# A chunked state-space scan that feeds a two-layer product: chunks of 64 tokens instead of 128, weight conversion on three engines, second product two groups behind

## The chip, the core and the metric

One core of a Trainium2 chip runs the whole program. TensorE (PE in the profile; PEld is its weight load) multiplies, VectorE (DVE), ScalarE (ACT) and GpSimd (POOL) work elementwise, and SyncE (SP) issues most of the DMA transfers. The metric is the device time of one execution in microseconds, lower is better.

## The reference

The first half is a scan with a decaying state (batch 4, 8 heads, 768 tokens, 32 channels per head, 16 states), here for one head:

```python
cum = np.cumsum(np.log(a))                       # within a chunk
M = (C @ B.T) * exp(cum[i] - cum[j]) * (i >= j)
y = M @ x + (C @ state) * exp(cum)
state = exp(cum[-1]) * state + (B * exp(cum[-1] - cum)).T @ x
```

The heads of a token are put side by side, which gives 3072 tokens of 256 channels, and the second half is a product with SiLU between its two layers:

```python
h = y @ w_in                   # 256 -> 2048
out = (h / (1 + exp(-h))) @ w_out   # 2048 -> 256
```

The result does not depend on the length of the chunks. All inputs are fp32 except the two weight matrices, which reach the chip as float64 and are rounded to fp32 on it. All products are fp32; the profile has two matmul records for each matmul instruction (one for each transpose).

## The kernel before, in words

Everything stays on the chip between the two halves. Tokens are worked on in groups of 256, twelve in all, three to a batch. The line numbers are those of the kernel before.

**The scan.** A group is two chunks of 128 tokens. Once per batch, `prep_decay` and `prep_T` bring B and C of 768 tokens into layouts with states on the partitions (`bh`, `ce`, `cw`), and `prep_N` brings B back to tokens on partitions (`bn`). B and C are loaded with six consecutive tokens on a partition, so GpSimd first sorts them (L224), PE transposes twelve blocks (L232), the copies put tokens in order, and six more transposes follow (L261). Per chunk there are four pieces. `f_E` (DVE, L268 and L271) makes the decays E between all pairs of tokens by one scan over 8 heads x 128 tokens on 128 partitions. `f_G` multiplies C and B for four pairs of heads on four row tiles of the PE array (L283), and DVE multiplies the result with E (M, L287). `f_D` forms the chunk's part of the state (L306, four column tiles), and DVE adds it to the decayed state and spreads it by a mask (L313, L317). `f_Y` multiplies the state (L326) and M (L334) into y, which ACT copies to XM (L339).

**The two layers.** `f_s1(g, j)` makes two of sixteen blocks of h (four matmuls, L352) in one of the two PSUM slots named `hp` and ACT applies SiLU (L354). `f_s2(g, j)` adds four of the sixteen blocks to an output tile (four matmuls, L361), and after each fourth call ACT copies the tile out (L365).

**The weights.** Sixteen pieces (eight of w_in, then eight of w_out) come in by DMA as pairs of 32-bit words. For each, `w_size` runs six instructions on DVE (L137 to L146) and one addition on GpSimd (L147), and `w_sign` one more on DVE (L153). Four pieces can be in flight; the load of piece n + 4 is issued after the last step of piece n.

**Order.** The order is written out by hand; no scheduler changes it, and each engine takes its instructions in program order. The loop at the end of the kernel runs over g = -1 to 12 and j = 0 to 7 and issues in each step: layer one of group g, preparation of a later batch, layer two of group g - 1, a piece of the scan of group g + 1, a piece of `f_E` or `f_B` of group g + 2, and, while g is below 1, the next weight piece. So all sixteen pieces are converted during g = -1 and g = 0, and layer one of group 0 shares DVE's queue with half of them.

Of the kernel before, what the change touches and what calls it, by code (L numbers as in the profile page):

```python
# [13 lines left out]
# as fp32, the bits of float64's high word for 2^-127 and for 2^128 * (1 - 2^-20)  # L14
# [5 lines left out]
def kernel(  # L20
# [22 lines left out]
    Q = 128  # L43
    CPB = S // Q
    NCH = batch * CPB
    R = S // 128
# [3 lines left out]
    GC = 2  # L50
    GT = GC * Q
    NG = NCH // GC
    GPB = CPB // GC
    assert (H * N, H * D, D, N) == (128, 256, 32, 16) and CPB % GC == 0 and d_model == H * D

    const = ctx.enter_context(tc.tile_pool(name="const", bufs=1))
    bcp = ctx.enter_context(tc.tile_pool(name="bcp", bufs=2))
    bcr = ctx.enter_context(tc.tile_pool(name="bcr", bufs=1))
    xp = ctx.enter_context(tc.tile_pool(name="xp", bufs=8))
    abp = ctx.enter_context(tc.tile_pool(name="abp", bufs=3))  # L60
    rawp = ctx.enter_context(tc.tile_pool(name="rawp", bufs=4))
    wtp = ctx.enter_context(tc.tile_pool(name="wtp", bufs=2))
    bat = ctx.enter_context(tc.tile_pool(name="bat", bufs=2))
    epool = ctx.enter_context(tc.tile_pool(name="epool", bufs=3))
    mpool = ctx.enter_context(tc.tile_pool(name="mpool", bufs=2))
    st = ctx.enter_context(tc.tile_pool(name="st", bufs=2))
    xmp = ctx.enter_context(tc.tile_pool(name="xmp", bufs=2))
    gpool = ctx.enter_context(tc.tile_pool(name="gpool", bufs=2))
    opool = ctx.enter_context(tc.tile_pool(name="opool", bufs=3))
    ps_g = ctx.enter_context(tc.tile_pool(name="ps_g", bufs=1, space=bass.MemoryType.PSUM))  # L70
    ps_y = ctx.enter_context(tc.tile_pool(name="ps_y", bufs=1, space=bass.MemoryType.PSUM))
    ps_h = ctx.enter_context(tc.tile_pool(name="ps_h", bufs=2, space=bass.MemoryType.PSUM))
    ps_o = ctx.enter_context(tc.tile_pool(name="ps_o", bufs=1, space=bass.MemoryType.PSUM))
# [4 lines left out]
    pa, bc, xt, ab = {}, {}, {}, {}  # L78
    RAW = 4

    def load_batch(b, q0, q1):
        # a of a batch, each head on the N partitions of its states
        pa[b] = bat.tile([128, S], FP32, name="pa")
        q0.dma_start(out=pa[b], in_=bass.AP(tensor=a.tensor, offset=a.offset + b * H * S,
                                            ap=[[S, H], [0, N], [1, S]]))
        # token p * R + r of a batch on partition p: runs of R * N elements
        bc[b] = bcp.tile([128, 2, H, R * N], FP32, name="bc")
        for i, q in ((0, q0), (1, q1)):
            q.dma_start(out=bc[b][:, i], in_=(B, C)[i][b].rearrange("h (p r) n -> p h (r n)", r=R))

    def load_a(gc):
        # a of a chunk on all partitions
        b, c = divmod(gc, CPB)
        ab[gc] = abp.tile([128, H, Q], FP32, name="ab")
        nc.sync.dma_start(out=ab[gc], in_=bass.AP(tensor=a.tensor, offset=a.offset + b * H * S + c * Q,
                                                  ap=[[0, 128], [S, H], [1, Q]]))

    def load_x(gc):
        b, c = divmod(gc, CPB)
        xt[gc] = xp.tile([128, H, D], FP32, name="xt")  # L100
        nc.sync.dma_start(out=xt[gc], in_=x[b, :, c * Q:(c + 1) * Q, :].rearrange("h p d -> p h d"))
# [6 lines left out]
    raw = {}  # L108

    def w_piece(which, j):  # L110
# [4 lines left out]
    def load_w(which, j, q):  # L115
        src, dst = w_piece(which, j)
        if src.dtype == FP32:
            q.dma_start(out=dst, in_=src)
            return
        t = raw[which, j] = rawp.tile([128, 2, 2 * WF], U32, name="raw")  # L120
        q.dma_start(out=t, in_=src.bitcast(U32))

    # float64 as (low, high) words to fp32
    def w_parts(n):
        w = raw[W[n]].rearrange("p k (f two) -> p k f two", two=2)
        return w[:, :, :, 0], w[:, :, :, 1]

    def w_size(n):
        if W[n] not in raw:
            return  # L130
        lo, hi = w_parts(n)
        t = wt[n] = wtp.tile([128, 2, WF], U32, name="wt")
        r = wtp.tile([128, 2, WF], U32, name="wr")
        tf, rf = t.bitcast(FP32), r.bitcast(FP32)
        # the high word's magnitude orders as an fp32 number of its bits, so comparing it as one holds
        # it in fp32's range of exponents: below comes zero, above the largest numbers
        nc.vector.tensor_scalar(out=t, in0=hi, scalar1=0x7FFFFFFF, scalar2=None, op0=ALU.bitwise_and)  # L137
# [3 lines left out]
        nc.vector.tensor_scalar(out=t, in0=t, scalar1=4, scalar2=1,  # L141
                                op0=ALU.logical_shift_left, op1=ALU.logical_shift_right)
        nc.vector.tensor_scalar(out=t, in0=t, scalar1=0x40000000, scalar2=None, op0=ALU.bitwise_xor)  # L143
        # the low word's part: low * 2^-52 of the power of two
        nc.vector.tensor_scalar(out=r, in0=t, scalar1=0x7F800000, scalar2=None, op0=ALU.bitwise_and)  # L145
        nc.vector.scalar_tensor_tensor(out=rf, in0=lo, scalar=2.0 ** -52, in1=rf, op0=ALU.mult, op1=ALU.mult)  # L146
        nc.gpsimd.tensor_tensor(out=tf, in0=tf, in1=rf, op=ALU.add)  # L147

    def w_sign(n):
        if W[n] in raw:  # L150
            lo, hi = w_parts(n)
            dst = w_piece(*W[n])[1]
            nc.vector.scalar_tensor_tensor(out=dst.bitcast(U32), in0=hi, scalar=0x80000000, in1=wt.pop(n),  # L153
                                           op0=ALU.bitwise_and, op1=ALU.bitwise_or)
        if n + RAW < len(W):
            load_w(*W[n + RAW], nc.sync)
# [288 lines left out]
```

## Time and profile before

| | us |
|---|---|
| median of three runs | 487.18 (486.95 to 487.48) |
| span of the profiled execution, first to last instruction | 484.2 |
| median of the runs above that span | 3.0 |
| PE busy | 410.2 (85% of the span) |
| DVE busy | 207.2 (43%) |
| ACT busy | 87.7 (18%) |
| POOL busy | 60.6 (13%) |

The profile is of one execution, whose own time is known as its span; what lies around the span (3.0 us, if this execution was a median one) is carried unchanged through the prediction. Busy shares are averages over the span: what an engine is worth is read from the stage in which it is the last to finish. Times are in microseconds unless marked ns. In a row of the timeline the first number is the start from the span's start, the second how long the group of instructions lasted, and `xN` the number of records in it.

### The profile page before, as it was taken

The numbers are of one execution on the slowest core, as the hardware profiler recorded it, in microseconds if no ns is written. First come the engines' busy times: TensorE is split into PE (matmuls) and PEld (weight loads), VectorE is DVE, ScalarE is ACT, GpSimd is POOL, SyncE is SP. The second block draws the span as 40 slices with busy tenths as digits, with TensorE's granted clock in tenths as the row PEclk, the third lists the DMA queues.
The fourth block names the chain that finished last, engine by engine and source line by source line (L and its number), as shares of the span: only waits on it lengthen the run. The fifth ranks groups of instructions, "written<-read, shape, count | busy, mean of one in ns | idle before, by whom it ended". The sixth has DMA issues, their size and how long they took to land.

```text
span 484.2 us, 5726 instructions
## 1 busy us (share of the span) xinstructions
PE 410.2 (85%) x2424; PEld 333.0 (69%) x2424; DVE 207.2 (43%) x258; ACT 87.7 (18%) x162; POOL 60.6 (13%) x89
## 2 busy tenths in 40 slices
PE   0421816456999999999999999999999999999996
PEld 0210514345887787888878888888878778788885
DVE  2999999997703414528034036172250341100000
ACT  1200201011221121122212212222112121212110
POOL 6022342234200000300100003002000000000000
PEclk9999969597999999999999999999999999999999
DMA  9994434310271302202704022022010000000000
GB/s 195 272 242 136 131 111 126 125 51 1 70 159 35 88 11 67 54 12 65 153 12 110 21 54 66 12 65 56 11 56 11 1 12 11 11 2 12 11 12 22
DMA packets 66617, 32.35 MB, mean 67 GB/s; under 512 B 34336, under 2 KB 61984, under 8 KB 66592
## 3 DMA queue, kind: packets, MB, share of 16 engines
q1 hardware_dynamic: 65552, 31.59, 25.3%
q10 hardware_dynamic: 1040, 0.39, 0.3%
q8 instruction: 19, 0.31, 0.3%
q14 instruction: 6, 0.05, 0.0%
HBM read 28.84 MB, written 3.15 MB: 66 GB/s over the span
## 4 chain that ended last, share of the span: by engine, by line
PE 76%; DVE 18%; issue 2%; DMA 2%; POOL 1%; ACT 0%; SPq 0%; ACTq 0%; POOLq 0%
PE o_ps L361 34%; PE hp L352 33%; DVE E L271 3%; DVE wt L137 3%; PE gram L283 3%; PE yb L334 2%; PE yb L326 2%; DMA bc<-in_B_dram 2%; DVE wt L138 2%; DVE wr L145 1%; DVE wt L141 1%; DVE wt L143 1%; DVE w_in_sb L153 1%; DVE SP L317 1%; DVE w_out_sb L153 1%
## 5 line engine op out<-in xcount | busy, mean ns | idle before, releaser
L352 PE MATMUL hp<-XM,w_in_sb 128*128 128x256 f32 x768 | 191.8, 394 | 0.5 <-ACT XM L339 0.5
L361 PE MATMUL o_ps<-w_out_sb,gT 128*128 128x256 f32 x768 | 181.7, 381 | 1.0 <-ACT o_sb L365 1.0
L352 PEld LDWEIGHTS hp<-XM,w_in_sb 128*128 128x128 f32 x768 | 143.5, 193 | 32.5 <-issue 9.0
L361 PEld LDWEIGHTS o_ps<-w_out_sb,gT 128*128 128x128 f32 x768 | 145.4, 191 | 21.1 <-ACT o_sb L365 1.8
L354 ACT ACTIVATE gT<-hp 128x512 f32<-128x512 f32 x96 | 57.3, 597 | 231.3 <-PE hp L352 231.3
L287 DVE TENSOR_TENSOR M<-gram,E 128x1024 f32<-128x1024 f32 x24 | 29.3, 1219 | 162.8 <-PE gram L283 162.8
L271 DVE TENSOR_TENSOR_SCAN E<-ab,ident 128x1024 f32<-128x1024 f32 x24 | 56.6, 2358 | 5.8 <-POOL ab L269 5.8
L326 PE MATMUL yb<-cw,SP 128*128 128x128 f32 x80 | 14.0, 302 | 38.5 <-DVE SN L313 38.5
L326 PEld LDWEIGHTS yb<-cw,SP 128*128 128x128 f32 x80 | 13.0, 211 | 40.4 <-DVE SN L313 39.5
L269 POOL MEMSET ab<- 128x8 f32 x24 | 2.7, 112 | 252.9 <-DVE ab L268 252.9
L147 POOL TENSOR_TENSOR wt<-wt,wr 128x512 f32<-128x512 f32 x16 | 25.1, 1566 | 57.3 <-DVE wr L146 57.3
L232 PE MATMUL hp<-ident,br 128*128 128x128 f32 x48 | 9.0, 325 | 20.7 <-POOL br L224 20.4
L339 ACT ACTIVATE XM<-yb 128x256 f32<-128x256 f32 x24 | 9.2, 383 | 95.4 <-PE yb L334 95.4
L232 PEld LDWEIGHTS hp<-ident,br 128*128 128x128 f32 x48 | 6.9, 166 | 22.4 <-POOL br L224 20.8
L334 PE MATMUL yb<-M,xt 128*32 128x128 f32 x384 | 17.2, 302 | 5.9 <-DVE SN L311 5.9
L283 PE MATMUL gram<-ce,bh 32*128 32x256 f32 x192 | 18.7, 460 | 0.0
L365 ACT ACTIVATE o_sb<-o_ps 128x256 f32<-128x256 f32 x24 | 9.2, 383 | 41.7 <-PE o_ps L361 39.4
L334 PEld LDWEIGHTS yb<-M,xt 128*32 128x32 f32 x384 | 9.9, 117 | 9.9 <-DVE SN L311 6.1
L268 DVE TENSOR_SCALAR ab<-ab 128x1024 f32<-128x1024 f32 x24 | 16.4, 684 | 0.4 <-DMA ab<-in_a_dram 0.4
L248 DVE TENSOR_SCALAR ce<-hp,par 128x256 f32<-128x256 f32 (+1 forms) x16 | 12.7, 875 | 6.1 <-PE hp L232 6.1
L296 POOL TENSOR_TENSOR BT<-bn,E 128x128 f32<-128x128 f32 x20 | 13.4, 678 | 10.7 <-DVE SN L313 6.9
L137 DVE TENSOR_SCALAR wt<-raw 128x512 uint32<-128x512 uint32 x16 | 14.2, 890 | 0.3
(36 smaller groups left out, 144.8 us busy)
## 6 DMA issues: line engine op xcount, KB each, us to landing
ab<-in_a_dram SPq DMA_DIRECT2D x24, 512.0 KB, 4.1
raw<-in_moe_w_in_dram SPq DMA_DIRECT2D x8, 512.0 KB, 5.1
raw<-in_moe_w_out_dram SPq DMA_DIRECT2D x8, 512.0 KB, 3.6
xt<-in_x_dram SPq DMA_DIRECT2D x24, 128.0 KB, 4.1
out_dram<-o_sb SPq DMA_DIRECT2D x24, 128.0 KB, 1.7
pa<-in_a_dram SPq DMA_DIRECT2D x4, 384.0 KB
bc<-in_B_dram SPq DMA_DIRECT2D x4, 384.0 KB, 8.3
bc<-in_C_dram SPq DMA_DIRECT2D x3, 384.0 KB, 8.5
```

Of the source, the lines that this page charges most:

```text
L137: nc.vector.tensor_scalar(out=t, in0=hi, scalar1=0x7FFFFFFF, scalar2=None, op0=ALU.bitwise_and)
L147: nc.gpsimd.tensor_tensor(out=tf, in0=tf, in1=rf, op=ALU.add)
L232: nc.tensor.transpose(out=tp[:, s * 128:(s + 1) * 128], in_=d["br"][:, i, r].rearrange("p h n -> p (h n)"), identity=ident)
L268: nc.vector.tensor_scalar(out=t, in0=t, scalar1=1.0, scalar2=1e-6, op0=ALU.min, op1=ALU.max)
L271: nc.vector.tensor_tensor_scan(out=E[gc].rearrange("p h t -> p (h t)"), data0=t.rearrange("p h t -> p (h t)"), data1=ident8.rearrange("p h ...
L283: nc.tensor.matmul(out=gram[:, g, 0:256], lhsT=d["bh"][32 * g:32 * g + 32, cs], rhs=d["ce"][32 * g:32 * g + 32, :, cs], start=True, stop=True,
L287: nc.vector.tensor_tensor(out=M[gc], in0=gram[:, :, 0:256], in1=E[gc].rearrange("p (g e) t -> p g (e t)", e=2), op=ALU.mult)
L326: nc.tensor.matmul(out=y_ps[:, w], lhsT=sp[:, w * 128:(w + 1) * 128], rhs=U[b]["cw"][:, c * Q:(c + 1) * Q], start=(w == 0), stop=False, sk ...
L334: nc.tensor.matmul(out=y_ps[32 * k:32 * k + 32, w], lhsT=xc[:, h], rhs=m[:, h], start=(c == 0 and w == 0), stop=True, tile_position=(0, 32 ...
L352: nc.tensor.matmul(out=hp[:, i * GT:(i + 1) * GT], lhsT=w_in_sb[:, kc, f * 128:(f + 1) * 128], rhs=XM[g][:, kc, :], start=(kc == 0), stop= ...
L354: nc.scalar.activation(GTS[g][:, 2 * j:2 * j + 2].rearrange("p f t -> p (f t)"), hp, AF.Silu)
L361: nc.tensor.matmul(out=OPS[g], lhsT=GTS[g][:, f, tt * Q:(tt + 1) * Q], rhs=w_out_sb[:, f, :], start=(f == 0), stop=(f == NF - 1))
```

## The change

The whole scan and the weight conversion are rewritten; the two layers keep their matmuls.

- **Chunks of 64 tokens.** A unit of 256 tokens is four chunks; two chunks lie one above the other on the partitions (64 c, c = 0 or 1), two beside each other (k). `f_E` makes E for a unit with one scan over 2 x 8 x 64 elements, where the kernel before had two scans over 8 x 128. Each matmul of `f_G`, `f_D` and `f_Y` is cut in smaller ones: 16, 16 and 16 + 32 for a unit, with 64 or 128 columns, on tiles of 32 x 64 or 64 x 32 of the PE array.
- **Natural order.** B and C are loaded per unit with one token on a partition (runs of 64 bytes), so that four transposes per unit suffice (`f_T`); the sorting on GpSimd, the six transposes back and the per-batch preparation are gone. The copies behind the transposes move from DVE to ACT, but for `cw`.
- **Loads.** One unit is eleven DMAs, issued as a block by `load_unit` two units ahead. Of unit 0, B, C and x come through ACT's queue.
- **Weights.** Per piece two instructions on ACT, two on GpSimd and two on DVE, spread over three successive steps (`w_size`, `w_bits`, `w_sign`); five pieces can be in flight.
- **Order.** Layer two runs two groups behind layer one (LAG = 2). Unit 0 is scanned before the loop with pieces 0 to 3; the other pieces follow, one per step, until j = 5 of g = 1.
- **PSUM.** `gram` and `y` share four banks under one name (`gy`), `f_D` takes both `hp` slots, and the output tile has two slots instead of one.

```diff
-    Q = 128
+    Q = 64
+    UT = 256
...
+    LAG = 2
...
+    gpool = ctx.enter_context(tc.tile_pool(name="gpool", bufs=LAG + 1))
...
+        for t in range(4):
+            k, c = divmod(t, 2)
+            q.dma_start(out=ab[u][64 * c:64 * c + 64, k],
+                        in_=bass.AP(tensor=a.tensor, offset=a.offset + b * H * S + t0 + t * Q,
+                                    ap=[[0, 64], [S, H], [1, Q]]))
...
+            for k in range(2):
+                q.dma_start(out=bct[u][:, i, k],
+                            in_=(B, C)[i][b, :, t0 + 128 * k:t0 + 128 * k + 128].rearrange("h p n -> p h n"))
...
+            nc.scalar.activation(u, raw[n][:, :, :, 1].bitcast(FP32), AF.Abs)
...
+            nc.scalar.activation(v, raw[n][:, :, :, 0], AF.Copy, scale=2.0 ** -51, bias=2.0)
...
+            nc.gpsimd.tensor_scalar(out=u, in0=u, scalar1=LEAST, scalar2=MOST, op0=ALU.max, op1=ALU.min)
...
+    def w_bits(n):
...
+            nc.vector.tensor_scalar(out=u, in0=u, scalar1=3, scalar2=None, op0=ALU.logical_shift_left)
+            nc.gpsimd.tensor_tensor(out=v, in0=u, in1=v, op=ALU.add)
...
+            nc.vector.scalar_tensor_tensor(out=dst.bitcast(U32), in0=raw[n][:, :, :, 1], scalar=0x80000000,
+                                           in1=wv.pop(n).bitcast(U32), op0=ALU.bitwise_and, op1=ALU.bitwise_or)
...
+        if n < len(W):
+            w_size(n)
+        if 0 <= n - 1 < len(W):
+            w_bits(n - 1)
+        if 0 <= n - 2 < len(W):
+            w_sign(n - 2)
...
+        nc.scalar.activation(BH[u], tb, AF.Copy)
+        for e in range(2):
+            nc.scalar.activation(CE[u][:, e], tcc, AF.Copy, scale=par[:, e:e + 1])
+        nc.vector.tensor_tensor(out=CW[u], in0=tcc, in1=PFX[u], op=ALU.mult)
...
+                for g in range(4):
+                    nc.tensor.matmul(out=gram[64 * c:64 * c + 64, g, 128 * k:128 * k + 128],
+                                     lhsT=bh[32 * g:32 * g + 32, ts], rhs=ce[32 * g:32 * g + 32, :, ts],
+                                     start=True, stop=True, tile_position=(32 * g, 64 * c), skip_group_check=True)
...
+        dp = [ps_h.tile([128, 512], FP32, name="hp") for c in range(2)]
...
+                nc.tensor.matmul(out=dp[c][32 * g:32 * g + 32, 64 * k:64 * k + 64],
+                                 lhsT=bt[64 * c:64 * c + 64, k, 32 * g:32 * g + 32],
+                                 rhs=xc[64 * c:64 * c + 64, k, 64 * g:64 * g + 64], start=True, stop=True,
+                                 tile_position=(64 * c, 32 * g), skip_group_check=True)
...
+                nc.tensor.matmul(out=y[64 * q:64 * q + 64, 2 * w + c, 64 * k:64 * k + 64],
+                                 lhsT=sp[32 * g:32 * g + 32, t], rhs=cw[32 * g:32 * g + 32, Q * t:Q * t + Q],
...
+                        nc.tensor.matmul(out=y[32 * q:32 * q + 32, 2 * w + c, 64 * k:64 * k + 64],
+                                         lhsT=xc[64 * c:64 * c + 64, k, h], rhs=m[64 * c:64 * c + 64, k, h],
...
+    def scan_piece(u, j):
+        if j == 0:
+            f_P(u)
+            f_E(u)
+        elif j == 1:
+            f_T(u)
+            f_B(u)
+        elif j == 2:
+            f_G(u)
+        elif j == 4:
+            f_D(u)
         elif j == 6:
...
+            f_Y(u)
+        elif j == 7 and u + 2 < NU:
+            load_unit(u + 2)
...
+    for g in range(NU + LAG):
         for j in range(8):
...
+            if g < NU:
                 f_s1(g, j)
...
+                scan_piece(g + 1, j)
+            if 8 * g + j + 4 < len(W) + 2:
+                next_w(8 * g + j + 4)
+            if g >= LAG:
+                f_s2(g - LAG, j)
```

On PE, one group in the loop's steady part stood like this before (a row is the line, the tile written and the tiles read with their buffer numbers, the size of one, and the count of instructions; L352 is layer one, L361 layer two, the rest is the scan):

```order
L352 MATMUL hp_960<-XM_861,w_in_sb_111 128x256 x4
L361 MATMUL o_ps_966<-w_out_sb_112,gT_801 128x256 x4
L283 MATMUL gram_161<-ce_632,bh_631 128x256 x4
L352 MATMUL hp_977<-XM_861,w_in_sb_111 128x256 x4
L361 MATMUL o_ps_966<-w_out_sb_112,gT_801 128x256 x4
L306 MATMUL yb_162<-xt_463,BT_942 32x64 x4
L352 MATMUL hp_1001<-XM_861,w_in_sb_111 128x256 x4
L361 MATMUL o_ps_966<-w_out_sb_112,gT_801 128x256 x4
L326 MATMUL yb_162<-cw_633,SP_907 128x128 x2
L334 MATMUL yb_162<-M_975,xt_463 32x128 x8
```

The same place now, from j = 3 to j = 6 of a group (L339 is layer one, L350 layer two; `hp_887` and `hp_888` are the two slots of `f_D`):

```order
L339 MATMUL hp_867<-XM_770,w_in_sb_87 128x256 x4
L350 MATMUL o_ps_809<-w_out_sb_88,gT_317 128x256 x4
L339 MATMUL hp_881<-XM_770,w_in_sb_87 128x256 x4
L278 MATMUL hp_887<-xt_566,BT_832 32x64 x4
L278 MATMUL hp_888<-xt_566,BT_832 32x64 x4
L278 MATMUL hp_887<-xt_566,BT_832 32x64 x4
L278 MATMUL hp_888<-xt_566,BT_832 32x64 x4
L350 MATMUL o_ps_913<-w_out_sb_88,gT_317 128x256 x4
L339 MATMUL hp_918<-XM_770,w_in_sb_87 128x256 x4
L350 MATMUL o_ps_913<-w_out_sb_88,gT_317 128x256 x4
L339 MATMUL hp_928<-XM_770,w_in_sb_87 128x256 x4
L313 MATMUL gy_934<-cw_827,sp_911 64x64 x12
```

What a group ran as two rounds of three pieces is now one round of larger pieces with many more, smaller matmuls, and the state's piece stands directly behind a layer-one block and takes the `hp` slot that this block has just filled.

On DVE, one weight piece stood like this before, between the pieces ahead of and behind it (`wt` and `wr` are its work tiles, `raw` what came by DMA):

```order
L137 TENSOR_SCALAR wt_348<-raw_289 128x512
L138 TENSOR_SCALAR wt_348<-wt_348 128x512
L141 TENSOR_SCALAR wt_348<-wt_348 128x512
L143 TENSOR_SCALAR wt_348<-wt_348 128x512
L145 TENSOR_SCALAR wr_349<-wt_348 128x512
L146 SCALAR_TENSOR_TENSOR wr_349<-raw_289,wr_349 128x512
L153 SCALAR_TENSOR_TENSOR w_in_sb_111<-raw_265,wt_323 128x2x256
```

DVE's rows around the same pieces now (`wu` and `wv` are the work tiles; L249 is `cw`, L262 is M):

```order
L146 TENSOR_SCALAR wu_292<-wu_292 128x512
L152 SCALAR_TENSOR_TENSOR w_in_sb_87<-raw_123,wv_236 128x2x256
L249 TENSOR_TENSOR cw_356<-hp_349,pfx_327 128x256
L146 TENSOR_SCALAR wu_333<-wu_333 128x512
L152 SCALAR_TENSOR_TENSOR w_in_sb_87<-raw_125,wv_293 128x2x256
L262 TENSOR_TENSOR M_396<-gy_379,E_331 128x4x2x128
```

Five of seven instructions per piece have left DVE, and those that stay wait for GpSimd. On GpSimd, where a piece had been one addition, the rows from the scan's product L231 on are now:

```order
L231 TENSOR_TENSOR BT_361<-bct_115,E_331 128x256
L141 TENSOR_SCALAR wu_363<-wu_363 128x512
L147 TENSOR_TENSOR wv_334<-wu_333,wv_334 128x512
L141 TENSOR_SCALAR wu_398<-wu_398 128x512
L147 TENSOR_TENSOR wv_364<-wu_363,wv_364 128x512
```

GpSimd had one instruction of a piece, and has two: it takes the clamp of one piece and then the addition of the piece before it.

More of the change, by code (lines that the diff above doesn't have):

```diff
@@ L107, with w_piece @@
     WF = 256
-    raw = {}
-    def w_piece(which, j):
+    W = [("i", j) for j in range(8)] + [("o", j) for j in range(8)]
+    RAW = 5
+    raw, wu, wv = {}, {}, {}
+    def w_piece(n):
+        which, j = W[n]
         if which == "i":
@@ new lines, in scan_piece @@
+    def scan_piece(u, j):
[9 more added lines that the diff above has]
+            f_D(u)
+        elif j == 6:
+            f_Y(u)
+        elif j == 7 and u + 2 < NU:
+            load_unit(u + 2)
+    f_P(0)
+    f_E(0)
+    f_T(0)
+    f_B(0)
+    next_w(0)
+    f_G(0)
+    next_w(1)
+    f_D(0)
+    next_w(2)
+    f_Y(0)
+    next_w(3)
+    load_unit(2)
```

439 lines of the change are left out of this document (174 added, 265 removed).

## The prediction

> **What bounds the kernel now.** I read the slices of the page first, then busy time by stretch, then PE's timeline in one steady group. The slices:
>
> ```profile
> PE   0421816456999999999999999999999999999996
> ...
> DVE  2999999997703414528034036172250341100000
> ...
> PEclk9999969597999999999999999999999999999999
> ```
>
> DVE is full for about nine slices of 12 us, then PE is full to the end. The stretches, cut at the first layer-one matmul and at the first layer-two matmul (columns: length, busy time and records of PE, PEld, DVE, ACT, POOL, then granted clock, DMA share, GB/s):
>
> ```profile
> 0.00:49.40 49.40, 11.32 (x86) 6.75 (x86) 38.74 (x54) 4.22 (x7) 14.97 (x24) 1.00 0.88 213
> 49.40:114.20 64.80, 33.26 (x173) 24.42 (x174) 60.27 (x95) 8.40 (x14) 23.72 (x22) 0.80 0.32 97
> 114.20:480.90 366.70, 365.65 (x2167) 301.80 (x2165) 108.17 (x111) 74.75 (x141) 21.92 (x44) 1.00 0.17 42
> 480.90:484.20 3.30, 0.00 (x0) 0.00 (x0) 0.00 (x0) 0.38 (x1) 0.00 (x0) 1.00 0.12 40
> ```
>
> So there are two bounds, one behind the other. In 49.40:114.20 DVE is busy 60.27 of 64.80 and PE half of it; in 114.20:480.90 PE is busy 365.65 of 366.70 at clock 1.00, and nothing but less PE work or an earlier start helps. The steady group on PE (start, length, line, records):
>
> ```profile
> 207.54 1.89 PE L352 MATMUL hp<-XM,w_in_sb 128*128 128x256 f32 x8
> 209.27 1.89 PE L361 MATMUL o_ps<-w_out_sb,gT 128*128 128x256 f32 x8
> 211.09 0.71 PE L283 MATMUL gram<-ce,bh 32*128 32x256 f32 x8
> 211.73 1.99 PE L352 MATMUL hp<-XM,w_in_sb 128*128 128x256 f32 x8
> 213.56 0.60 PE L232 MATMUL hp<-ident,br 128*128 128x128 f32 x4
> 214.00 1.89 PE L361 MATMUL o_ps<-w_out_sb,gT 128*128 128x256 f32 x8
> 215.82 0.32 PE L306 MATMUL yb<-xt,BT 128*32 128x64 f32 x8
> 216.07 1.99 PE L352 MATMUL hp<-XM,w_in_sb 128*128 128x256 f32 x8
> ...
> 220.07 0.61 PE L326 MATMUL yb<-cw,SP 128*128 128x128 f32 x4
> 220.60 0.65 PE L334 MATMUL yb<-M,xt 128*32 128x128 f32 x16
> 221.18 1.99 PE L352 MATMUL hp<-XM,w_in_sb 128*128 128x256 f32 x8
> 223.01 0.60 PE L232 MATMUL hp<-ident,br 128*128 128x128 f32 x4
> ```
>
> Starts count here, since lengths overlap. A block of four matmuls takes 1.73 (207.54 to 209.27), 0.216 a record. From 114.2 on, 183 of the 192 blocks remain: 316.6. The other 50.1 is the scan of ten groups, 5.0 each. Piece by piece, with the 0.10 by which the block behind is longer (211.73 to 213.56 is 1.83): `f_G` 0.83 (0.09 of it before its first record), transposes 0.44, `f_D` 0.44, `f_Y` 1.21.
>
> **The change on PE.** All 192 blocks stay. A unit's scan has 32 records in `f_G` (128 columns), 32 in `f_D` and 96 in `f_Y` (64 columns), and four transposes. The nearest rows for a small tiled record are L306, 8 records of 64 columns from 215.82 to 216.07, 0.031 each, and L334, 16 of 128 columns from 220.60 to 221.18, 0.036 each. With 0.031 for 64 columns and 0.036 for 128: `f_G` 1.15 + 0.19 at its ends = 1.34; `f_D` 0.99 + 0.19; `f_Y` 2.98 + 0.10 = 3.08; transposes 0.44. No row shows tiles of 32 x 64 or 64 x 32, so both ends stand: from below the weight loads of L334, 16 in 0.38, 0.024 a record:
>
> ```profile
> 199.95 0.38 PEld L334 LDWEIGHTS yb<-M,xt 128*32 128x32 f32 x16
> ```
>
> and from above records that do not overlap at all, 0.216 x 64/256 = 0.054 and 0.108. That is 1.3 less or 5.2 more per unit.
>
> The Trainium skill speaks against such a cut: "TensorEngine Tiling (Array Packing)", Performance Considerations, gives each matmul an overhead of about 60 cycles and advises against tiling a dimension that is already small. By its figure at the skill's 2.4 GHz a record has a floor of 25 ns, an estimate of 4.0 for a unit's 160 records instead of 5.1, and a sum 10 lower than mine; the 31 ns of L306, with its ends in it, lies above that floor and agrees.
>
> `f_D` also waits. It takes both `hp` slots behind a layer-one block that has filled one:
>
> ```profile
> 197.69 1.89 PE L361 MATMUL o_ps<-w_out_sb,gT 128*128 128x256 f32 x8
> 197.89 0.60 ACT L354 ACTIVATE gT<-hp 128x512 f32<-128x512 f32 x1 [3.30 <-PE hp L352]
> ```
>
> The block before L361 stopped issuing at 197.69, its SiLU ended at 198.49, 0.80 later. `f_D` has 0.36 of start and first chunk to hide it, so 0.5 stays with the signal. Behind it in PE's queue is layer two of the same step, which has nothing to do with the slot and waits all the same. The next layer-one block needs the slot from which DVE reads the state; 1.73 of layer two covers that, and in g = 0 and 1, where layer two is absent, it costs 1.2 a group, in a stage that PE does not bound (below). Sum per unit 6.5, less 8 records in two of three units: 6.4. From g = 2 on nine units (3 to 11) are scanned: 58. Blocks from g = 2 on: 80 + 96 = 176, 304.5. Layer two of the last two groups runs alone, which is the same work. Edits that I cost at nothing: the three copies behind the transposes that go to ACT (each shorter than a SiLU, ACT is busy 74.75 of 366.70), and the eleven loads of a unit that stand ahead of a store on SP's queue, since for a store only the third output tile after it waits; without that cover the copies would cost 1.8 a unit.
>
> **The change on DVE and GpSimd.** Weight pieces before:
>
> ```profile
> 99.45 0.68 DVE L153 SCALAR_TENSOR_TENSOR w_out_sb<-raw,wt 128x512 uint32<-128x512 uint32 x1
> 99.67 1.58 POOL L147 TENSOR_TENSOR wt<-wt,wr 128x512 f32<-128x512 f32 x1 [3.00 <-DVE wr L146]
> 100.17 1.38 DVE L137 TENSOR_SCALAR wt<-raw 128x512 uint32<-128x512 uint32 x1
> ...
> 104.12 0.68 DVE L153 SCALAR_TENSOR_TENSOR w_out_sb<-raw,wt 128x512 uint32<-128x512 uint32 x1
> ```
>
> A piece takes 4.67 (99.45 to 104.12). The addition and DVE's instructions exclude each other: L147, started at 99.67, ends 1.12 after L153 does (101.25 against 100.13), and L137, whose like take 0.43, lasts until 0.30 after L147. The same is stated by the Trainium skill, "SBUF — State Buffer", Who interferes with whom: DVE instructions with two SBUF inputs or in a 2-port mode and GpSimd lock one port pair against each other. The trace agrees; without that rule a piece would cost GpSimd's own 1.8 and PE would bound the start.
>
> The prices from rows:
>
> ```profile
> L271 DVE TENSOR_TENSOR_SCAN E<-ab,ident 128x1024 f32<-128x1024 f32 x24 | 56.6, 2358 | 5.8 <-POOL ab L269 5.8
> L268 DVE TENSOR_SCALAR ab<-ab 128x1024 f32<-128x1024 f32 x24 | 16.4, 684 | 0.4 <-DMA ab<-in_a_dram 0.4
> L317 DVE TENSOR_TENSOR SP<-SN,bmask 128x256 f32<-128x256 f32 x20 | 12.5, 625 | 0.7
> L215 DVE TENSOR_TENSOR_SCAN pfx<-pa,pb 128x768 f32<-128x768 f32 x4 | 8.8, 2191 | 2.3 <-POOL pa L213 2.3
> L141 DVE TENSOR_SCALAR wt<-wt 128x512 uint32<-128x512 uint32 x16 | 6.8, 427 | 0.6
> L182 POOL TENSOR_SCALAR_AFFINE_SELECT ident<-ident 128x1024 f32<-128x1024 f32 x1 | 1.1, 1091 | 0.1
> L190 POOL TENSOR_SCALAR_AFFINE_SELECT bmask<-bmask 128x256 f32<-128x256 f32 x1 | 0.4, 444 | 0.1
> ```
>
> A piece now holds the pair for a clamp on GpSimd (not in the trace; 0.66 between the two selects of 256 and 1024 elements, 1.12 if it is as slow as the addition), the addition 1.12 (an integer one; taken as the fp32 one), the shift 0.43 and the sign 0.68: 2.9, at most 3.4. ACT's two instructions, 0.6 each like a SiLU, lie beside it. A unit's scan holds the pair for E 2.36, its clamp 0.68, prefixes 0.73 (a third of L215), spread 0.63, and about 1.4 for BT and small ones: 5.8.
>
> The start: ab lands, then E.
>
> ```profile
> 10.95 0.74 DVE L268 TENSOR_SCALAR ab<-ab 128x1024 f32<-128x1024 f32 x1 [0.43 <-DMA ab<-in_a_dram]
> ...
> 49.83 3.78 PE L352 MATMUL hp<-XM,w_in_sb 128*128 128x256 f32 x8 [0.50 <-ACT XM L339]
> ```
>
> I keep 11 for it. E ends at 14.2, M 15.4, the state and its spread about 18; PE then runs at half pace, as the 3.78 of its first block shows, so `f_Y` takes 5.5 and XM is there at 24, not at 49. But the third weight piece lies behind two units and two pieces in the queues: 3.9 MB (1.18 a unit, 0.52 a piece) at the 213 GB/s of the first stretch, from 1.6 on: 20. From there 14 pieces and two units hold the pair 14 x 2.9 + 11.6 = 52, to 72. PE alone would reach g = 2 at 24 + 2 x (13.8 + 6.4) and 2 for slow blocks: 66. What ties them is ACT: its two instructions for piece 15 stand ahead of SiLU (1, 4) and need the tile of piece 12, free at 72 - 3 x 2.9 = 63.5. After that 1.8 on ACT, `f_D` 1.7, three blocks 5.2 and `f_Y` 3.1 follow: g = 2 starts at 76 (66 to 83).
>
> The load is more packets:
>
> ```profile
> q1 hardware_dynamic: 65552, 31.59, 25.3%
> ```
>
> that is 30 ns a packet on one of 16 engines. A unit has 8320 packets (4096 of 64 bytes); at 30 ns that is 15.6, under the 34 of a steady group, and at the start up to 10 later than bytes alone say. I take bytes, since short packets cannot cost more than the mean of long ones, and keep the 10.
>
> **The sum.** 76 + 304.5 + 58 = 438.5 for PE's end; 3.3 for the last copy and store, as in 480.90:484.20, and 0.4 for issuing the store in two; span 442.2, and 3.0 around it: 445.2, against 487.18.
>
> **The rivals.**
> 1. *Small tiles run one after the other on PE.* If records of different tiles do not overlap in the new shapes, a unit costs 5.2 more, nine units 47, and the time is 492: slower. It decides when the mean record reaches 0.061 (42 / 9 / 160 above 0.032). Against it: L283, L306 and L334 all overlap now; for it, none has both sides cut. 0.07.
> 2. *The conversion keeps its old pace.* DVE's order puts signs and shifts ahead of `cw` and M, and each waits for GpSimd; at 4.67 a piece the last sign comes at 97, that of piece 12 at 83, and g = 2 at 95: 464. For it: the exclusion. Against: only 2.9 of work holds the pair. 0.16.
> 3. *PE binds from the start and small records run at their weight-load pace.* g = 2 at 66 and 0.024 a record: 445 - 10 - 11 = 424. For it: the clamp may be short and L306's 0.031 has ends in it. 0.20.
> 4. The forecast, 435 to 458: 0.57.
>
> **How the numbers follow.** 445 is the forecast's own sum. 427 leaves out the best half of rival 3 (0.08), 468 rival 1 and the worst of rival 2 with late loads (0.11). Slower by over 0.2% (about what a measurement of this kernel can tell from no change) is rival 1: 0.07; within 0.2% needs a record within 0.001 of 0.061: 0.01; the rest, 0.92, is faster.
>
> **What would show it.** Right: first layer-one block near 24, layer two from about 76, sixteen signs about 2.9 apart, blocks at 1.73 after that, 96 records of `f_Y` in about 3.1, and an idle 0.5 on PE at L278 behind SiLU. The forecast is wrong if layer two starts after 85 (then the conversion or the loads), or if a unit's scan adds over 8 on PE (then the tiles).

## The result, and the profile after

| | before | after |
|---|---|---|
| median, us | 487.06 (486.55 to 487.48, four runs) | 433.85 (433.72 to 434.53, four runs) |
| ratio of the times | | 0.891 [0.890, 0.893] |
| profiled execution's own time | | 433.9 |
| its span | 484.2 | 432.2 |

53 us are gone. The forecast was 445 in a range of 427 to 468, so side and size hold, 11 us too high. Those 11 us are the rest of two larger errors of opposite sign, which the slices of the page after show only roughly:

```profile
PE   2255785799999999999999999999999999999996
...
DVE  1728868813212213113014014014014011000000
...
POOL 4567988500000000000000000000000000000000
```

DVE is no longer full over nine slices: in slices 4 to 8 it has 6 to 8 tenths and GpSimd 5 to 9, and PE is full from slice 9 on. The stretches, cut at the first layer-one block, at the start of g = 2 and at PE's end, give the sizes (columns as before):

```profile
0.00:26.50 26.50, 5.51 (x156) 3.63 (x156) 9.59 (x16) 6.49 (x12) 11.96 (x23) 1.00 1.00 201
26.50:86.90 60.40, 42.60 (x448) 33.09 (x449) 46.42 (x54) 28.41 (x51) 50.15 (x40) 0.92 0.66 150
86.90:428.80 341.90, 337.19 (x2838) 287.19 (x2836) 57.80 (x93) 71.98 (x141) 9.12 (x33) 1.00 0.19 34
```

Layer one of g = 2 begins at 86.9, where 76 was forecast (66 to 83). The 176 blocks and nine scans behind it take 341.9, where 304.5 + 58 = 362.5 was forecast. The steady unit on PE shows where the second difference lies:

```profile
123.85 0.60 PE L239 MATMUL hp<-ident,bct 128*128 128x128 f32 x4
124.29 1.89 PE L350 MATMUL o_ps<-w_out_sb,gT 128*128 128x256 f32 x8
126.02 1.89 PE L339 MATMUL hp<-XM,w_in_sb 128*128 128x256 f32 x8
127.84 0.69 PE L258 MATMUL gy<-ce,bh 32*64 32x128 f32 x32
128.46 1.99 PE L350 MATMUL o_ps<-w_out_sb,gT 128*128 128x256 f32 x8
...
135.56 0.32 PE L278 MATMUL hp<-xt,BT 64*32 64x64 f32 x8
136.32 0.43 PE L278 MATMUL hp<-xt,BT 64*32 64x64 f32 x24 [0.44 <-ACT gT L341]
136.68 1.99 PE L350 MATMUL o_ps<-w_out_sb,gT 128*128 128x256 f32 x8
...
143.78 0.69 PE L313 MATMUL gy<-cw,sp 32*64 32x64 f32 x32
144.41 0.86 PE L322 MATMUL gy<-M,xt 64*32 64x64 f32 x64
145.19 1.99 PE L350 MATMUL o_ps<-w_out_sb,gT 128*128 128x256 f32 x8
...
155.66 0.60 PE L239 MATMUL hp<-ident,bct 128*128 128x128 f32 x4
```

The blocks have not changed: 124.29 to 126.02 is 1.73. A unit lasts 31.81 (123.85 to 155.66), 4.13 more than its sixteen blocks. In it `f_G` has 32 records in 0.62 (127.84 to 128.46, 0.019 each), `f_Y` 32 in 0.63 and then 64 in 0.78 (144.41 to 145.19, 0.012 each), and `f_D` takes 1.12 with its wait of 0.44.

The time of before is accounted for in three pieces. Steady PE work now begins 27.3 earlier (86.9 against 114.2). By then PE has done 16 blocks, not 9, so that 7 x 1.73 = 12.1 less remains. The scans behind that point take 341.9 - 304.5 = 37.4 instead of 50.1, 12.7 less. Together 52.1, and the spans differ by 52.0.

The earlier stretch is that of the weights. In its middle, GpSimd's timeline reads:

```profile
49.30 2.09 POOL L141 TENSOR_SCALAR wu<-wu 128x512 f32<-128x512 f32 x1
51.36 1.28 POOL L147 TENSOR_TENSOR wv<-wu,wv 128x512 uint32<-128x512 uint32 x1
52.60 2.09 POOL L141 TENSOR_SCALAR wu<-wu 128x512 f32<-128x512 f32 x1
54.67 1.27 POOL L147 TENSOR_TENSOR wv<-wu,wv 128x512 uint32<-128x512 uint32 x1
```

and DVE's beside it:

```profile
50.28 0.68 DVE L152 SCALAR_TENSOR_TENSOR w_in_sb<-raw,wv 128x512 uint32<-128x512 uint32 x1
51.42 1.50 DVE L146 TENSOR_SCALAR wu<-wu 128x512 uint32<-128x512 uint32 x1 [0.46 <-POOL wu L141]
52.84 1.09 DVE L152 SCALAR_TENSOR_TENSOR w_in_sb<-raw,wv 128x512 uint32<-128x512 uint32 x1
```

GpSimd goes from clamp to addition without a gap, a piece every 3.31 (51.36 to 54.67). DVE waits for it, 0.46 ahead of its shift. The third piece's load is late as well. SP's queue ahead of it:

```profile
8.24 0.65 SPq L78 DMA_DIRECT2D pa<-in_a_dram  x1
...
19.38 11.07 SPq L128 DMA_DIRECT2D raw<-in_moe_w_in_dram  x5
```

and the rows of the two engines that wait for it:

```profile
24.84 0.66 ACT L136 ACTIVATE wu<-raw 128x512 f32<-128x512 f32 x1 [8.94 <-DMA raw<-in_moe_w_in_dram]
25.58 1.91 POOL L141 TENSOR_SCALAR wu<-wu 128x512 f32<-128x512 f32 x1 [6.42 <-ACT wu L136]
```

SP issues the eleven loads of unit 1 from 8.24 to 19.38, and only then the third piece, which is there 5.5 later. ACT stands 8.94 for it, GpSimd 6.42. The copy of unit 0's y to XM (25.95) stands behind it on ACT, so PE, which had y at 21.6, waits 5.03 and starts layer one at 26.58, where 24 was forecast.

### The profile page after: what moved, and what is told of

Its sections match the earlier page's. It is cut to its first block, busy times and chain, and to the rows that moved or that the text cites. A ratio compares the mean times of both kernels' runs of the same rounds, so it can differ in the third digit from the quotient of the medians.

```text
span 432.2 us, 7900 instructions
## 1 busy us (share of the span) xinstructions
PE 385.3 (89%) x3440; PEld 323.9 (75%) x3440; DVE 113.8 (26%) x162; ACT 106.9 (25%) x202; POOL 71.2 (16%) x95
## 4 chain that ended last, share of the span: by engine, by line
PE 79%; POOL 9%; DMA 4%; SPq 2%; issue 2%; ACT 2%; ACTq 1%; DVE 1%; POOLq 0%; DVEq 0%
PE o_ps L350 40%; PE hp L339 34%; POOL wu L141 6%; POOL wv L147 3%; PE gy L322 2%; DMA xt<-in_x_dram 2%; PE gy L313 1%; PE gy L258 1%; ACT gT L341 1%; DMA raw<-in_moe_w_in_dram 1%; SPq L93 1%; PE hp L239 1%; PE hp L278 1%; DMA ab<-in_a_dram 1%; ACTq L93 1%
## 5 line engine op out<-in xcount | busy, mean ns | idle before, releaser
L339 PE MATMUL hp<-XM,w_in_sb 128*128 128x256 f32 x768 | 187.9, 390 | 20.2 <-DVE w_in_sb L152 6.2
L339 PEld LDWEIGHTS hp<-XM,w_in_sb 128*128 128x128 f32 x768 | 149.4, 196 | 43.7 <-issue 9.5
L350 PE MATMUL o_ps<-w_out_sb,gT 128*128 128x256 f32 x768 | 181.7, 383 | 0.0
L350 PEld LDWEIGHTS o_ps<-w_out_sb,gT 128*128 128x128 f32 x768 | 143.0, 190 | 21.2 <-issue 1.5
L249 DVE TENSOR_TENSOR cw<-hp,pfx 128x256 f32<-128x256 f32 x12 | 5.0, 421 | 124.0 <-ACT ce L248 124.0
L141 POOL TENSOR_SCALAR wu<-wu 128x512 f32<-128x512 f32 x16 | 32.8, 2054 | 6.4 <-ACT wu L136 6.4
L223 DVE TENSOR_TENSOR_SCAN E<-ab,diag 128x1024 f32<-128x1024 f32 x12 | 28.3, 2355 | 2.6 <-POOL ab L221 2.6
L293 DVE SCALAR_TENSOR_TENSOR st<-st,pfx,hp 128x64 f32<-128x64 f32 x40 | 11.2, 281 | 43.5 <-PE hp L278 41.8
L147 POOL TENSOR_TENSOR wv<-wu,wv 128x512 uint32<-128x512 uint32 x16 | 21.3, 1333 | 3.2 <-DVE wu L146 3.2
L262 DVE TENSOR_TENSOR M<-gy,E 128x1024 f32<-128x1024 f32 x12 | 14.7, 1223 | 24.6 <-PE gy L258 24.6
L146 DVE TENSOR_SCALAR wu<-wu 128x512 uint32<-128x512 uint32 x16 | 16.8, 1053 | 12.4 <-POOL wu L141 12.4
L278 PE MATMUL hp<-xt,BT 64*32 64x64 f32 x352 | 8.5, 234 | 9.9 <-ACT gT L341 6.5
L136 ACT ACTIVATE wu<-raw 128x512 f32<-128x512 f32 x16 | 10.7, 669 | 16.1 <-DMA raw<-in_moe_w_in_dram 12.7
L239 PE MATMUL hp<-ident,bct 128*128 128x128 f32 x48 | 8.2, 288 | 6.9 <-DMA bct<-in_B_dram 4.0
L138 ACT ACTIVATE wv<-raw 128x512 f32<-128x512 uint32 x16 | 10.6, 666 | 8.7 <-DVE w_out_sb L152 5.6
```

What stands on the lines that cost most here:

```text
L141: nc.gpsimd.tensor_scalar(out=u, in0=u, scalar1=LEAST, scalar2=MOST, op0=ALU.max, op1=ALU.min)
L146: nc.vector.tensor_scalar(out=u, in0=u, scalar1=3, scalar2=None, op0=ALU.logical_shift_left)
L147: nc.gpsimd.tensor_tensor(out=v, in0=u, in1=v, op=ALU.add)
L223: nc.vector.tensor_tensor_scan(out=E[u].rearrange("p k h t -> p (k h t)"), data0=t.rearrange("p k h t -> p (k h t)"), data1=diag.rearrange ...
L239: nc.tensor.transpose(out=tp[:, 2 * i + k], in_=bct[u][:, i, k].rearrange("p h n -> p (h n)"), identity=ident)
L262: nc.vector.tensor_tensor(out=M[u].rearrange("p k g x -> p g k x"), in0=gram[:, :, 0:256].rearrange("p g (k x) -> p g k x", k=2), in1=E[u] ...
```

## The experiments

The theory after the result had two halves. PE's half: records of different tiles run beside one another, so the cut scan is cheap. The head's half: the conversion, by GpSimd's two instructions and the late loads, sets when g = 2 starts. The rivals: small records are simply cheap whatever their tile; the scan, not the conversion, held the start; the order of the loads is hidden anyway.

Times below are medians of four runs. Ratios are to the kernel before, run on the same chip, with a 95% interval; after has 0.891 [0.890, 0.893] and 433.85. Where the steady stretch is as long as that of after, 341.90, the whole difference lies in the head.

**Layer two one group behind.** `LAG` is 1, and the pieces are converted two a step in g = 0.

```diff
-    LAG = 2
+    LAG = 1
...
-            if 8 * g + j + 4 < len(W) + 2:
-                next_w(8 * g + j + 4)
+            if g == 0:
+                next_w(2 * j + 4)
+                next_w(2 * j + 5)
```

> Layer two runs one group behind layer one instead of two, and in exchange two weight pieces are taken per step of group 0, so that all are there when layer two begins. Theory: during the conversion PE then has only layer one of group 0 to do, and group 1 starts at about 75 us with 184 blocks and ten units ahead of it: 75 + 318 + 41 + 5 = 440 us, 6 us slower. Rival (the lag is not what gives PE work, the conversion alone is): 434 us.

Measured: 436.94 (436.22 to 437.55), ratio 0.897 [0.896, 0.899]: 3.1 slower than after. PE in g = 0:

```profile
51.08 0.44 PE L278 MATMUL hp<-xt,BT 64*32 64x64 f32 x8 [4.40 <-POOL wu L141]
57.61 0.65 PE L278 MATMUL hp<-xt,BT 64*32 64x64 f32 x24 [6.08 <-ACT gT L341]
```

Layer two begins 15.6 earlier, at 73.10 against 88.71, but with less layer-one work before it, and `f_D` stands 4.40 and 6.08 behind conversions that are now twice as dense in the queues of GpSimd and ACT. The lag, together with the slower pace of conversion that it allows, is worth 3 of the 53 us: with it the conversions have two groups of layer one to lie beside, not one. The edit changes both at once, so neither has a price of its own.

**The clamp on DVE.**

```diff
-            nc.gpsimd.tensor_scalar(out=u, in0=u, scalar1=LEAST, scalar2=MOST, op0=ALU.max, op1=ALU.min)
+            nc.vector.tensor_scalar(out=u, in0=u, scalar1=LEAST, scalar2=MOST, op0=ALU.max, op1=ALU.min)
```

> The clamp of a weight piece goes from GpSimd to DVE; nothing else changes. Theory A: GpSimd paces the start, with a clamp of 1.9 to 2.1 us and an addition of 1.24 us per piece (3.3 us). Then a piece costs the pair of DVE and GpSimd 1.24 + 0.43 + 0.43 + 0.68 = 2.8 us, fourteen pieces end 7 us earlier, and the time is about 427 us. Theory B: the loads pace the start (the third piece was there at 24.8 us only, and each later one waits for a transfer). Then the time stays at 434 us, within 1.

Measured: 431.20 (430.16 to 432.58), ratio 0.886 [0.883, 0.888]: 2.7 faster. Where the data is there, a piece now takes 2.34:

```profile
72.27 1.55 POOL L147 TENSOR_TENSOR wv<-wu,wv 128x512 uint32<-128x512 uint32 x1 [0.79 <-DVE wu L146]
74.61 1.55 POOL L147 TENSOR_TENSOR wv<-wu,wv 128x512 uint32<-128x512 uint32 x1 [0.79 <-DVE wu L146]
```

One less per piece would be 14 over the pieces that are left. Only 3.7 of that reaches PE (g = 2 at 83.2, with a steady stretch of 341.90, in an execution 1.0 shorter than the median). The time lies between the two theories, 427 and 434. The group of ACT's first step shows what is late next:

```profile
L136 ACT ACTIVATE wu<-raw 128x512 f32<-128x512 f32 x16 | 10.8, 672 | 18.5 <-DMA raw<-in_moe_w_in_dram 14.8 <-DMA raw<-in_moe_w_out_dram 3.7
```

All of its 18.5 of idle time are loads (15.6 in after, and 0.5 for GpSimd). So GpSimd's clamp is a bound, and the loads lie close behind it.

**Pieces 2 to 4 loaded ahead of unit 1.** The line numbers of this kernel are two lower.

```diff
-    for n in range(2):
+    for n in range(RAW):
         load_w(n, nc.sync)
     load_unit(1)
-    for n in range(2, RAW):
-        load_w(n, nc.sync)
```

> The weight pieces 2 to 4 are loaded ahead of unit 1 instead of behind it. Theory B (the loads pace the start): the third piece lands 6 to 8 us earlier, GpSimd's idle 6.4 us before its third clamp goes, and the time falls by 5 to 6 us, to 428. Theory A (GpSimd's pace alone counts): the idle time is part of the same chain, so some of it is won too, but unit 1 comes 5 us later and its scan takes the gain back in GpSimd's and DVE's queues: 432 to 435 us.

Measured: 430.33 (428.93 to 431.44), ratio 0.884 [0.881, 0.886]: 3.5 faster. GpSimd's wait of 6.42 for the third clamp is gone:

```profile
18.37 1.26 POOL L147 TENSOR_TENSOR wv<-wu,wv 128x512 uint32<-128x512 uint32 x1
19.60 2.02 POOL L141 TENSOR_SCALAR wu<-wu 128x512 f32<-128x512 f32 x1
```

The third clamp starts 6.0 earlier, but g = 2 only 2.5 (84.4). Part is given back to a later load: ACT waits 2.53 for a piece at 41.48. The time lies between the two theories here as well. So the loads' order was not hidden, and neither was it the only bound.

**The state's products in banks of their own.** `f_D` writes a four-bank `gy` tile and not both `hp` slots. The lines behind it are one higher.

```diff
-        dp = [ps_h.tile([128, 512], FP32, name="hp") for c in range(2)]
+        gd = ps_s.tile([128, 4, 512], FP32, name="gy")
+        dp = [gd[:, c] for c in range(2)]
```

> The state's matmuls write the four-bank tile that the product of C and B has left, instead of both slots of layer one. Theory: the 0.44 us by which PE waits for the SiLU in each unit goes and nothing takes its place: nine units win 4.0 us in the steady part, and the waits of units 1 and 2 for these slots (0.4, 1.2, 2.2 and 2.4 us) are hidden behind the conversion, so about 430 us. Rival: the new tile makes y or the product of the next unit wait for DVE, and the time stays at 434 us or rises.

Measured: 425.17 (424.56 to 426.00), ratio 0.874 [0.872, 0.876]: 8.7 faster, where 4 were expected from the wait alone. PE's timeline at the piece:

```profile
101.11 0.45 PE L279 MATMUL gy<-xt,BT 64*32 64x64 f32 x32
101.49 1.99 PE L351 MATMUL o_ps<-w_out_sb,gT 128*128 128x256 f32 x8
```

and the steady stretch:

```profile
84.10:419.60 335.50, 334.79 (x2838) 286.24 (x2836) 60.76 (x95) 71.96 (x141) 9.35 (x35) 1.00 0.20 35
```

The piece takes 0.38 instead of 1.12. The 0.44 that the trace of after calls a wait is not all that the shared slot cost: the eight records ahead of the wait took 0.32 from 135.56 and the rest could start only at 136.32. The steady stretch is 6.4 shorter with the same 2838 records (0.7 a unit), and g = 2 starts 2.8 earlier (84.1).

**Neighbouring matmuls on one tile.** The second part of `f_Y` has its 32 matmuls in another order, so that four in a row (eight records) use the same tile of the array. The same matmuls write the same places.

```diff
-        for k in range(2):
-            for w in range(2):
-                for c in range(2):
-                    for q in range(4):
+        for c in range(2):
+            for q in range(4):
+                for k in range(2):
+                    for w in range(2):
```

> The 32 matmuls of the scan's last product keep their number, operands and tiles, but the four that share a tile of the PE array now stand one behind another, where each neighbour had another tile. Theory: these small records cost only 0.012 us because neighbours run on different tiles at once; records on one tile follow each other at 64 columns' own pace, 0.054 us, so a unit costs 64 x 0.042 = 2.7 us more, nine units 24 us: about 458 us. Rival: the price is set by how fast PE takes instructions, whatever the tile: 434 us.

Measured: 452.90 (450.30 to 455.25), ratio 0.930 [0.925, 0.935]: 19.05 slower, from the order of 32 matmuls per unit. PE's timeline there:

```profile
117.61 0.58 PE L313 MATMUL gy<-cw,sp 32*64 32x64 f32 x24
118.11 2.40 PE L322 MATMUL gy<-M,xt 64*32 64x64 f32 x64
120.45 1.99 PE L350 MATMUL o_ps<-w_out_sb,gT 128*128 128x256 f32 x8
```

and the steady stretch:

```profile
92.40:448.20 355.80, 351.13 (x2838) 301.12 (x2836) 57.19 (x92) 71.97 (x141) 8.48 (x32) 1.00 0.18 33
```

The group of those records over the whole span (busy time, mean ns of one):

```profile
L322 PE MATMUL gy<-M,xt 64*32 64x64 f32 x768 | 30.5, 227 | 0.0
```

In after, the same group reads:

```profile
L322 PE MATMUL gy<-M,xt 64*32 64x64 f32 x768 | 10.6, 231 | 0.0
```

The mean duration of one record is the same (227 and 231 ns; the ends of matmul records are modelled), but 64 of them take 2.34 instead of 0.78: 0.037 each, not 0.012. Nine rounds of 1.56 make 14.0, and the steady stretch is 13.9 longer. The other 5.5 lie ahead of g = 2 (92.4 against 86.9), where the third clamp is also 1.5 later (27.11); they are not taken apart. So a record is cheap because its neighbours are on other tiles, and the rival, cheap whatever the tile, falls.

The single records' starts in the two traces say how. In after, eight start 0.007 apart from 144.41, and the next eight follow from 144.49 at the same pace: a round over the tiles every 0.06 to 0.08. Here only five start from 118.12 to 118.36, the last four 0.056 apart, which is the expected 0.054 of a tile that works alone. Later the starts are 0.025 to 0.031 apart, as of two such rows beside each other, so the mean is 0.037 and the expected time was too long. The new order also changes which PSUM bank follows which; the 0.056 speaks for the tile, but no run separates the two.

**The kernel before, with the new conversion alone.** ACT, GpSimd and DVE share the conversion as in the change; `w_bits` and the later sign come along, and three pools are resized so that it fits (x 6 buffers instead of 8, work tiles 3 instead of 2, output 2 instead of 3).

```diff
-        nc.vector.tensor_scalar(out=t, in0=hi, scalar1=0x7FFFFFFF, scalar2=None, op0=ALU.bitwise_and)
-        nc.vector.tensor_scalar(out=tf, in0=tf, scalar1=MOST, scalar2=LEAST, op0=ALU.min, op1=ALU.max)
...
-        nc.gpsimd.tensor_tensor(out=tf, in0=tf, in1=rf, op=ALU.add)
+        nc.scalar.activation(u, hi.bitcast(FP32), AF.Abs)
+        nc.scalar.activation(v, lo, AF.Copy, scale=2.0 ** -51, bias=2.0)
+        nc.gpsimd.tensor_scalar(out=u, in0=u, scalar1=LEAST, scalar2=MOST, op0=ALU.max, op1=ALU.min)
```

> The kernel before, with the new conversion of the weights alone (three engines, three steps per piece, three work buffers; x in six buffers and the output in two instead of eight and three to make room). Theory: about half of the 53 us won comes from the conversion; layer two of group 0 then starts at about 90 us instead of 114, and the time is about 463 us. Rival: the order of the kernel before, in which layer one of group 0 and half of the pieces share the steps, keeps PE waiting, and not more than 10 us are won: 477 us or more.

Measured: 468.00 (467.07 to 468.65), ratio 0.961 [0.959, 0.963]: 18.7 faster than before. Layer two begins at 81.33, 32.9 earlier, and then PE stops once more, as its timeline shows:

```profile
94.38 1.11 PE L224 MATMUL hp<-ident,br 128*128 128x128 f32 x4 [8.60 <-POOL br L216]
```

GpSimd's timeline ahead of that:

```profile
91.99 1.57 POOL L141 TENSOR_TENSOR wv<-wu,wv 128x512 uint32<-128x512 uint32 x1 [3.39 <-DVE wu L140]
93.51 1.59 POOL L216 COPY br<-bc 128x768 f32<-128x768 f32 x2
```

The sorting of B and C (L216 here) is queued on GpSimd behind the last addition, and PE's transposes wait 8.60 for it. That two instructions a piece on GpSimd pay in full only when the sorting has left it, as the natural order lets it, is what this wait suggests; no run takes the sorting alone away.

**The change with the old conversion.** The reverse of it: `w_size` has the six DVE instructions and the addition of before, and `w_bits` is empty.

```diff
-            nc.scalar.activation(u, raw[n][:, :, :, 1].bitcast(FP32), AF.Abs)
...
-            nc.gpsimd.tensor_scalar(out=u, in0=u, scalar1=LEAST, scalar2=MOST, op0=ALU.max, op1=ALU.min)
+        nc.vector.tensor_scalar(out=t, in0=hi, scalar1=0x7FFFFFFF, scalar2=None, op0=ALU.bitwise_and)
+        nc.vector.tensor_scalar(out=tf, in0=tf, scalar1=MOST, scalar2=LEAST, op0=ALU.min, op1=ALU.max)
...
+        nc.gpsimd.tensor_tensor(out=tf, in0=tf, in1=rf, op=ALU.add)
```

> The changed kernel with the conversion of the kernel before (seven instructions on DVE, one addition on GpSimd). Theory: pieces then come 4.7 us apart and wait for two units' scans on DVE, the last at about 105 us, layer two starts about 15 us later than now, and the time is about 449 us. Rival: two groups of lag hide the conversion whatever it costs: 434 to 438 us.

Measured: 454.65 (453.63 to 455.22), ratio 0.934 [0.932, 0.936]: 20.8 slower than after. Its stretches:

```profile
26.50:107.60 81.10, 45.07 (x448) 34.17 (x449) 73.61 (x121) 13.10 (x24) 26.05 (x26) 0.79 0.53 116
107.60:449.50 341.90, 337.15 (x2837) 287.15 (x2836) 57.19 (x92) 71.97 (x141) 8.47 (x32) 1.00 0.19 34
```

The steady stretch is 341.90, as in after; the head alone is 20.7 longer, with DVE busy 73.61 of 81.10. So the conversion is worth some 20 of the 53 us on either side (18.7 and 20.8), and the rest, 32 to 35, is left for the scan, its order and its loads together, which no run takes apart.

**Clamp, loads and banks together.** The edits of three of the experiments above in one kernel.

```diff
-            nc.gpsimd.tensor_scalar(out=u, in0=u, scalar1=LEAST, scalar2=MOST, op0=ALU.max, op1=ALU.min)
+            nc.vector.tensor_scalar(out=u, in0=u, scalar1=LEAST, scalar2=MOST, op0=ALU.max, op1=ALU.min)
...
-    for n in range(2):
+    for n in range(RAW):
...
-        dp = [ps_h.tile([128, 512], FP32, name="hp") for c in range(2)]
+        gd = ps_s.tile([128, 4, 512], FP32, name="gy")
+        dp = [gd[:, c] for c in range(2)]
```

> Three edits together: the clamp on DVE, weights loaded ahead of unit 1, the state's matmuls in the four-bank tile. Alone they won 2.7, 3.5 and 8.7 us against 433.85 us. If they are independent: 419 us. If clamp and loads each hid the other (each edit alone found the other wait next), the three win more than their sum: 414 to 417 us. If both only touch the same stretch: 421 to 423 us.

Measured: 418.38 (416.83 to 420.61), ratio 0.860 [0.857, 0.863]: 15.5 faster than after. It is the fastest of the kernels here. 433.85 - 2.7 - 3.5 - 8.7 = 419.0, so the medians fit gains that add, within a spread of 3.8 over the four runs. The profiled execution is the longest of them, 420.61. Its stretches:

```profile
26.50:80.10 53.60, 38.84 (x440) 30.30 (x439) 33.05 (x60) 25.14 (x46) 22.57 (x21) 0.87 0.83 179
80.10:415.50 335.40, 334.67 (x2837) 286.15 (x2835) 60.74 (x95) 71.96 (x141) 9.24 (x34) 1.00 0.20 35
```

In this execution g = 2 starts 6.8 earlier than in after, where the three edits alone gave 3.7, 2.5 and 2.8, together 9.0; so the head shows less than the sum. PE is busy 334.67 of 335.40 from 80.1 on, and ahead of that no engine is full: PE has 38.84 of 53.60, DVE 33.05, at a DMA share of 0.83. What still bounds the head is open; the DMA share points to the loads, and no run takes them away.

## Why the prediction was right, and where it was wrong

**Right: the two bounds and what stays.** PE is full from g = 2 on, at 1.73 a block, and of its 4.7 idle in 341.9 nine waits of `f_D` make 4.0. The edits costed at nothing, copies on ACT and eleven loads ahead of a store, can have cost no more than the other 0.7 there.

**Right: `f_D`'s wait.** 0.5 was forecast, 0.44 stands in the trace. The bank experiment adds that the shared slots cost 0.7 a unit in all, and 2.8 in the head, where they were to cost nothing, "in a stage that PE does not bound". That part was wrong.

**Wrong: the price of a record, in "the change on PE".** The sum took 0.031 for 64 columns and 0.036 for 128, with a lower end of 0.024. Measured are 0.019 (`f_G`, 128 columns), 0.020 and 0.012 (`f_Y`'s two parts). All lie below the lower end. No row of before had tiles cut on both sides, and 0.031 had the ends of a group of only eight records in it. `f_Y`'s first part goes round four tiles of the array and its second round eight, and the experiment with neighbours on one tile shows that for the second part this turn sets the price. A unit costs 37.4 / 9 = 4.2 instead of 6.4: 20.6 less than forecast, the largest error. The Trainium skill's overhead of about 60 cycles a matmul ("TensorEngine Tiling (Array Packing)", Performance Considerations) is not borne out here: by it a record could not fall below an estimated 25 ns, and the trace shows 12. Counted by instruction, of two records each, 12 would be 24, close to that floor; but with banks of its own `f_D` starts its 16 instructions between 101.11 and 101.35, 15 ns each. The Trainium skill's "TensorE: Matmul & The Clock Gate", Part 3, describes what does happen, matmuls of different tiles under way at the same time; there the trace agrees, with eight starts 0.007 apart.

**Wrong: the clamp on GpSimd, and with it the pace of 2.9.** The clamp was put between 0.66 and 1.12:

```profile
L141 POOL TENSOR_SCALAR wu<-wu 128x512 f32<-128x512 f32 x16 | 32.8, 2054 | 6.4 <-ACT wu L136 6.4
L147 POOL TENSOR_TENSOR wv<-wu,wv 128x512 uint32<-128x512 uint32 x16 | 21.3, 1333 | 3.2 <-DVE wu L146 3.2
```

It takes 2.05 on the mean, three times the 0.66 that was read off between two selects, and more than the addition. The pace is 3.3, so 14 pieces take 5.6 longer. The mechanism was another one as well. Not the exclusion between DVE and GpSimd sets the pace, but GpSimd's own 2.07 and 1.24, for the two DVE instructions lie beside them. The shift (L146, 51.42) does wait: it ends at 52.92, 0.28 after the addition. The sign (L152, 52.84 to 53.93), which reads two inputs from SBUF, runs while the clamp runs (52.60 to 54.69). It starts 0.24 after the clamp and takes 1.09 instead of 0.68. The sign at 50.28 also runs within a clamp (49.30 to 51.39), but starts 0.98 after it, and takes 0.68. So what stretches a sign lies near the clamp's start. The Trainium skill, "SBUF — State Buffer", Who interferes with whom, has this pair contend for the shared port. The trace agrees in that the first of these signs is slower, but it does not wait for the clamp's end, and the other is not slowed at all.

**Wrong: the third weight piece at 20.** It came at 24.84, 4.8 later. The bytes' 213 GB/s were about right (201 in the first stretch). Missing was that unit 1's eleven transfers hold SP's queue for 11.1 from 8.24 on, with the weights behind them. Whether SP's issuing or the transfers set these 11.1 is open: the DMA share is 1.03 meanwhile, one issue (12.22) follows on the landing of unit 0's x (12.21), and in the steady part the same eleven still take 7.9 (103.97 to 111.86). The prediction had kept up to 10 in its range for late loads, and the 4.8 lies inside that. In its own sum, 5.6 + 4.8 = 10.4 of the 10.9 by which g = 2 was late; past 85, as the prediction had said a wrong step would show, and the last sign ends at 83.05, not 72. The experiments do not give these amounts back one by one: 3.7 for the clamp, 2.5 for the loads, and each edit leaves the other waits in place, among them those for `f_D`'s slots (2.8).

**ACT's tie held in kind.** Near the end of the head, ACT's rows are:

```profile
73.74 0.66 ACT L136 ACTIVATE wu<-raw 128x512 f32<-128x512 f32 x1 [1.21 <-DMA raw<-in_moe_w_out_dram]
74.74 0.67 ACT L138 ACTIVATE wv<-raw 128x512 f32<-128x512 uint32 x1 [0.34 <-DVE w_out_sb L152]
75.31 0.57 ACT L341 ACTIVATE gT<-hp 128x512 f32<-128x512 f32 x1
```

SiLU stands behind the conversion's two instructions, and these wait for a load (1.21) and then for DVE (0.34). The prediction had named the queue and the second wait, for the tile of piece 12, whose sign ends at 74.71 (forecast 63.5); the wait for the load it had not. From there to g = 2 it is 12.2, where 12.5 was forecast.

**The sum.** 445.2 + 10.9 (late start) - 20.6 (cheap records) - 0.3 (end: 3.4, not 3.7) - 1.3 (1.7 around the span, not 3.0) = 433.9. (The steps listed up to g = 2 add up to 75.3; 76 was taken.) A forecast 2.6% off hid two terms that were off by 10.9 and 20.6, and that they have opposite signs is luck: with the cheap records and a start at 76, the sum would be 424.6, below the range. Of the rivals, tiles in series did not happen, nor did the old pace. The third, PE from the start with cheap records, was half right: the records were cheaper still, but PE did not bind from the start.

## What to carry to other kernels

Look at the order of small tiled matmuls before counting them: in turn over eight tiles, 64 records took 0.78, with eight in a row on one tile 2.34. When one engine's instruction is moved to another that has not run it, bound its price by more than the nearest-looking row, and ask which queue its data stands in. And when a wait for a shared buffer is short in the trace, take the buffer apart once: 0.44 of wait a unit was 0.7 of time.

## What the runs showed of the hardware

- A matmul record of 64 columns on a tile of 64 x 32 costs 0.012 us when its neighbours are on other tiles, 0.037 when eight in a row share one; its own modelled duration is 0.23 in both. Starts on different tiles come 0.007 apart, the first ones on one tile 0.056.
- GpSimd takes longer for a two-sided fp32 clamp of 512 elements a partition (1.91 with DVE idle, 2.05 on the mean) than for an integer addition of two such tiles (1.26). DVE takes 0.43 for the same clamp where nothing holds it up.
- A DVE instruction with two inputs in SBUF runs beside a GpSimd clamp. It took 1.09 instead of 0.68 when it started 0.24 after the clamp, and 0.68 when it started 0.98 after it.
